# Attention with two key tiles per cycle: maxima, scores, scores, maxima on TensorE

## The chip, the core and the metric

One core of one Trainium2 chip runs the whole program. The metric is the device time of one execution in microseconds (us). The engines are TensorE (PE, with its weight loads listed as PEld), VectorE (DVE), ScalarE (ACT), GpSimd (POOL) and SyncE (SP), which here issues every DMA. Each engine runs its own queue in order and waits on semaphores for the others.

## The reference

Block-sparse attention with 4 batches of 8 heads, 768 positions and a head size of 64, followed by a feed-forward layer over the 3072 tokens:

```python
scores = scale * np.matmul(q, k.transpose(0, 1, 3, 2))      # 768 x 768 per head
scores = np.where(mask, scores, -1000000000.0)              # window, first/last and sampled blocks of 32
scores = scores - np.max(scores, axis=-1, keepdims=True)
attn = np.exp(scores)
attn = attn / (np.sum(attn, axis=-1, keepdims=True) + 1e-09)
x = np.matmul(attn, v)                                      # heads side by side: 3072 x 512
h = x @ w_in                                                # 512 -> 2048
out = (h - np.tanh(h)) @ w_out                              # 2048 -> 512
```

## The kernel before

The 32 heads are worked in 16 pairs, since two heads of 64 fill 128 partitions. A head has six tiles of 128 keys. float32 accuracy comes from high and low parts (hi and lo), and the mask is put into the products by 24 more rows of the operands: `slot` buffers, three of them, hold keys and queries with those rows, and row 88 holds the negated maximum of each query.

For a pair, `prep_qk` transposes keys and queries on PE (`ptk`, `ptq`, L205), ACT makes the hi part (`hik`, `hiq`, L207), DVE the lo part (`lok`, `loq`, L208), and `dist` sends them into the slot by DMA (L220). `prep_v` scales the values: a maximum on DVE (`am`), a product on PE (`pa`, L240), three small DVE steps (`sb`), the hi part on ACT (`vhl`, L250) and the lo part on DVE (`vhl`, L251), which reads ACT's.

For a head, six calls of `smax` compute approximate scores with queries on partitions (`sm`, L265, two matmuls) and DVE reduces each to a column of `mc` (L269). `smax_fin` transposes `mc` on PE (`pmt`, L274), DVE negates it (`nm`, L276), and a DMA puts it into the slot (L277). Then come six calls of `qk_exp`: the exact scores with keys on partitions (`st`, four matmuls, L293 and L294; L294 reads the maxima), and the exponential on ACT (`pe`, L297). `split` makes a float16 hi part (`ph`, ACT L307, at two tiles of twelve DVE L305) and a lo part (`pl`, POOL L309, at one tile of twelve DVE). `accum` multiplies with the values, 18 small matmuls per tile (`av`, L324, L332, L333), always for two tiles in a row. `norm` divides (`rs`, `xq`), `spill` writes the pair to HBM.

All of `sm`, `st`, `ptk`, `ptq` live in one PSUM pool of three wide buffers (`ps_big`, two banks each). A tile gets one that is free at its place in the schedule, and which one is fixed in the built program. `pa`, `pmt` and `av` share two small ones.

The order of the work is a table of times: `at(time, f, ...)` enters each call with a time in units of one key tile, the list is sorted, and the calls are made in that order. A scheduler then orders each engine's queue; from head 5 on (`CH0`) a chain of dependencies, `in_order`, keeps `sm`, `st` and `av` on PE in the order of the calls. For key tile i = 6h + t, `qk_exp` stands at i, `smax` at i + TSM (up to one unit later in the first heads, `ramp`), `split` at i + 2.1, and the two `accum` of an even tile and its successor at i + 5.19 and i + 5.2. `smax` therefore runs ten tiles ahead, in the next pair of heads.

After the last pair the feed-forward part (class `FFN`) runs: `first` (L548), the activation, and `second` (L580 to L582).

Of the kernel before, what the change touches and what calls it, by code (L numbers as in the profile page):

```python
# [54 lines left out]
X0, DX = 175, 2  # L55


TQK, TV, TSM, LSP, LAV = -15.1, -5.6, -9.95, 2.1, 4.2
CH0 = 5
HPH, HPL = 29, 30  # L60
RS, RQ, RV, HR = 1, 2.5, 3, 6
# [15 lines left out]
@with_exitstack  # L77
def attention_ffn(ctx, tc, q, k, v, samp, w_in, w_out, blocks, out):
    nc = tc.nc
    cst = ctx.enter_context(tc.tile_pool(name="cst", bufs=1))  # L80
    dpool = ctx.enter_context(tc.tile_pool(name="dpool", bufs=1, space=DRAM))
    xscr = [dpool.tile([P, T, DM], F32, name=f"xscr{b}") for b in range(B)]

    ident = cst.tile([P, P], F32, name="ident")
    make_identity(nc, ident)
    bias = [cst.tile([P, 1], F32, name=f"bias{i}") for i in range(2)]
    for x, val in zip(bias, (QB, THR2)):
        nc.vector.memset(x, val)

    slots = [cst.tile([P, 4, 2, S], F32R, name=f"slot{i}") for i in range(NSLOT)]  # L90
    wt = {(m, ft): dpool.tile([P, 512], F32, name=f"w{m}{ft}") for ft in range(NPRE) for m in "io"}
    part = [dpool.tile([P, DM], F32, name=f"part{j}") for j in range(CT)]
    f2 = ctx.enter_context(tc.tile_pool(name="f2", bufs=2))
    stage = [cst.tile([P, 1024], I32, name=f"stage{i}") for i in range(2)]
    ffn = FFN(tc, w_in, w_out, xscr, ident, bias, slots, wt, out, f2, part, stage)
    with ExitStack() as actx:
        big = actx.enter_context(tc.tile_pool(name="ps_big", bufs=3, space=PSUM))
        one = actx.enter_context(tc.tile_pool(name="ps_one", bufs=2, space=PSUM))
        ps = (
            lambda name: big.tile([P, 1024], F32, tag="big", name=name),  # L100
            lambda name: one.tile([P, 512], F32, tag="one", name=name),
        )
        ffn.big, ffn.one = ps
        attention(actx, tc, q, k, v, samp, w_in, w_out, blocks, xscr, ident, ps, slots, wt, f2, ffn)
    with ExitStack() as fctx:
        ffn.rest(fctx)


def attention(ctx, tc, q, k, v, samp, w_in, w_out, blocks, xscr, ident, ps, slots, wt, f2, ffn):
# [247 lines left out]
    def ramp(h, by):  # L357

        return by * max(0, 1 - (h - 1) / HR) if h else 0

    def at(time, f, *args):
        ev.append((time, len(ev), f, args))
# [36 lines left out]
    for h in range(2 * NPAIR):  # L399
        tsm = TSM + ramp(h, RS)  # L400
        for t in range(T):
            i = 6 * h + t
            at(i + tsm, smax, h, t)
            at(i, qk_exp, h, t)
            at(i + LSP, split, h, t)
            at(i + LAV + PAIR * (1 - t % 2), accum, h, t)
        at(6 * h + tsm + 5.05, smax_fin, h)
        at(6 * h + 5 + LAV + 0.05, norm, h)
# [283 lines left out]
```

## Time and profile before

| | |
|---|---|
| three runs, median (lowest to highest) | 985.94 us (982.2 to 987.58) |
| the profiled execution's time | 984.79 us |
| its span, first to last instruction | 983.0 us |
| mean granted TensorE clock | 0.979 |
| busy: PE, PEld, DVE, ACT, POOL | 922.7, 770.8, 731.5, 630.0, 458.6 us |
| chain that ended last, share by engine | PE 73%, DMA 8%, ACT 6%, DVE 5% |
| first products of the feed-forward part | 429.92 us |

A row of a timeline is: start, duration, engine, line, operation, output<-inputs, shapes, count, and in brackets the idle time of the engine before it with what ended it. A matmul's duration includes its way through the array, so the time that it keeps PE is read from start to start. A row of waits is: who waited for whom, total us, times, longest. A row of the chain of waits is: start, duration, what.

### The profile page before, as it was taken

The page shows a single profiled execution, that of the slowest core. Times are in us where ns is not written, and L with a number is a line of the kernel's source. Part 1 is how long each engine was busy: PE and PEld are TensorE (multiplying, and loading weights), DVE is VectorE, ACT ScalarE, POOL GpSimd, SP SyncE. Part 2 cuts the span into 40 slices and gives each one's busy share as a digit, 9 for nine tenths or more (in the row PEclk, how much of TensorE's full clock was granted, in tenths as well). Part 3 has the DMA queues.
Part 4 walks back from the last instruction along what each step waited for, and adds up shares of the span by engine and source line. Part 5 has one row for each costly group of instructions (what it writes and reads, how often), then busy time and mean ns, then how long its engine had stood idle before and what let it go on. Part 6 is the DMA issues. An engine that isn't in the chain of part 4 may idle for free.

```text
span 983.0 us, 18553 instructions
## 1 busy us (share of the span) xinstructions
PE 922.7 (94%) x7264; PEld 770.8 (78%) x7264; DVE 731.5 (74%) x1120; ACT 630.0 (64%) x943; POOL 458.6 (47%) x308
## 2 busy tenths in 40 slices
PE   5789899999999999878999999999999999999997
PEld 3677788888887888767788888888888888888885
DVE  5679778888887888869999876765676666566664
ACT  1566878888888888665666665555555465555553
POOL 1556767777777777854445422222222222222221
PEclk9788999999999999998999999999999999999999
DMA  9896767777776767215451220210020000001001
GB/s 234 197 288 177 191 145 173 169 165 170 166 172 157 165 156 189 72 37 168 149 169 48 65 76 11 97 33 12 1 75 1 1 33 11 1 1 44 1 1 43
DMA packets 74695, 99.78 MB, mean 102 GB/s; under 512 B 6008, under 2 KB 63544, under 8 KB 74608
## 3 DMA queue, kind: packets, MB, share of 16 engines
q1 hardware_dynamic: 74608, 98.60, 38.5%
q8 instruction: 57, 0.93, 0.4%
q14 instruction: 30, 0.25, 0.1%
HBM read 44.64 MB, written 15.20 MB: 61 GB/s over the span
## 4 chain that ended last, share of the span: by engine, by line
PE 73%; DMA 8%; ACT 6%; DVE 5%; issue 4%; SPq 2%; POOL 1%; ACTq 0%; DVEq 0%; POOLq 0%
PE pf L548 25%; PE pf L580 9%; PE pf L581 8%; PE pf L582 8%; PE st L293 5%; PE st L294 5%; PE sm L265 4%; ACT pe L297 3%; DMA slot<-lok 2%; PE av L324 2%; PE av L332 2%; PE av L333 2%; DMA slot<-nm 2%; DMA rawi<-w_in 1%; SPq L220 1%
## 5 line engine op out<-in xcount | busy, mean ns | idle before, releaser
L309 POOL TENSOR_TENSOR pl<-pe,ph 128x768 f16<-128x768 f32 x173 | 290.4, 1693 | 130.9 <-ACT ph L307 63.8
L571 POOL TENSOR_TENSOR gl<-t,gh 128x512 fp32r<-128x512 f32 x96 | 124.3, 1295 | 357.4 <-ACT gh L570 305.3
L269 DVE TENSOR_REDUCE mc<-sm 128x1 f32<-128x768 f32 x192 | 181.1, 952 | 54.3 <-PE sm L265 51.5
L297 ACT ACTIVATE pe<-st 128x768 f32<-128x768 f32 x192 | 154.4, 806 | 81.6 <-PE st L294 71.2
L293 PE MATMUL st<-slot 128*128 128x512 f32 (+1 forms) x384 | 146.9, 383 | 17.6 <-ACT pe L297 13.4
L563 DVE TENSOR_TENSOR t<-t,pf 128x512 f32<-128x512 f32 x94 | 64.6, 688 | 122.8 <-ACT t L557 122.7
L570 ACT ACTIVATE gh<-t 128x512 fp32r<-128x512 f32 x96 | 60.6, 631 | 120.7 <-DVE t L567 120.7
L307 ACT ACTIVATE ph<-pe 128x768 f16<-128x768 f32 x154 | 130.0, 844 | 4.7
L294 PE MATMUL st<-slot 89*128 89x512 f32 (+1 forms) x384 | 126.8, 350 | 1.4 <-DMA slot<-nm 1.4
L265 PE MATMUL sm<-slot 88*128 88x512 f32 (+1 forms) x384 | 111.2, 376 | 11.1 <-DMA slot<-hiq 5.4
L324 PE MATMUL av<-vhl,ph 128*128 128x65 f16 x1152 | 120.8, 195 | 0.0
L333 PE MATMUL av<-vhl,pl 128*128 128x65 f16 x1152 | 119.6, 194 | 1.0 <-POOL pl L309 1.0
L332 PE MATMUL av<-vhl,ph 128*128 128x64 f16 x1152 | 119.8, 196 | 0.0
L324 PEld LDWEIGHTS <-ph 128*128 128x128 f16 x1152 | 106.8, 97 | 13.7 <-issue 13.0
L333 PEld LDWEIGHTS <-pl 128*128 128x128 f16 x1152 | 107.9, 100 | 3.1 <-issue 1.7
L332 PEld LDWEIGHTS <-ph 128*128 128x128 f16 x1152 | 108.0, 98 | 0.6 <-issue 0.5
L555 ACT ACTIVATE u<-pf 128x512 f32<-128x512 f32 x94 | 56.2, 598 | 81.3 <-PE pf L548 81.0
L293 PEld LDWEIGHTS st<-slot 128*128 128x128 f32 x384 | 75.3, 196 | 35.9 <-ACT pe L297 18.5
L294 PEld LDWEIGHTS st<-slot 89*128 89x128 f32 x384 | 75.9, 198 | 11.9 <-DMA slot<-nm 2.8
L265 PEld LDWEIGHTS sm<-slot 88*128 88x128 f32 x384 | 62.8, 203 | 18.9 <-issue 5.8
L567 DVE COPY_PREDICATED t<-mk,pf 128x512 f32<-128x512 int32 x94 | 69.9, 744 | 6.9 <-DVE pf L566 0.5
L581 PE MATMUL pf<-wx,gh 128*128 128x512 f32 x192 | 74.7, 389 | 0.0
(123 smaller groups left out, 1962.7 us busy)
## 6 DMA issues: line engine op xcount, KB each, us to landing
slot<-hik SPq DMA_DIRECT2D x64, 192.0 KB
slot<-hiq SPq DMA_DIRECT2D x64, 192.0 KB
stage<-w_in SPq DMA_DIRECT2D x13, 512.0 KB
stage<-w_out SPq DMA_DIRECT2D x13, 512.0 KB
rawk<-k SPq DMA_DIRECT2D x16, 384.0 KB
rawq<-q SPq DMA_DIRECT2D x16, 384.0 KB
slot<-lok SPq DMA_DIRECT2D x32, 192.0 KB
slot<-loq SPq DMA_DIRECT2D x32, 192.0 KB
```

Of the source, the lines that this page charges most:

```text
L265: nc.tensor.matmul(pm[:, c], lhsT=sB[s][0:88, j, t * P : (t + 1) * P], rhs=sA[s][0:88, j, c], start=True, stop=True)
L269: maxed.append(nc.vector.tensor_reduce(out=mcs[h][:, t : t + 1], in_=pm[:, 0:S], op=ALU.max, axis=AX.X))
L293: ms.append(nc.tensor.matmul(st[:, c], lhsT=sC[s][:, j, kc], rhs=sD[s][:, j, c], start=True, stop=False))
L294: ms.append(nc.tensor.matmul(st[:, c], lhsT=sA[s][0:89, j, kc], rhs=sB[s][0:89, j, c], start=False, stop=True))
L297: nc.scalar.activation(out=pe, in_=st[:, 0:S], func=AF.Exp, scale=0.125)
L307: nc.scalar.activation(out=ph, in_=pe, func=AF.Copy)
L309: d = eng.tensor_tensor(out=pl, in0=pe, in1=ph, op=ALU.subtract)
L324: m = nc.tensor.matmul(o[:, to, :], lhsT=ph[:, c], rhs=vv[:, 0:65], start=(kt == 0 and t == 0), stop=False, skip_group_check=True)
L332: nc.tensor.matmul(o[:, to, 0:64], lhsT=ph[:, c], rhs=vv[:, 65:129], start=False, stop=False, skip_group_check=True)
L333: m = nc.tensor.matmul(o[:, to, :], lhsT=pl[:, c], rhs=vv[:, 0:65], start=False, stop=last, skip_group_check=True)
L548: nc.tensor.matmul(h, lhsT=w[:, cc], rhs=x[:, c, :], start=(k == 0), stop=(k == 3 * NCT - 1))
L581: nc.tensor.matmul(o, lhsT=gh[:, c], rhs=wo[1][ft], start=False, stop=False)
```

## The change

Two numbers: TSM, which places `smax`, goes from -9.95 to -9.0, and odd tiles get 0.05 less, even ones 0.05 more. In a stretch of two key tiles the calls were scores, maxima, scores, maxima, products; now they are maxima, scores, scores, maxima, products, and each maximum, with `smax_fin` behind it, stands 0.95 later (0.9 or 1.0 by parity).

```diff
-TQK, TV, TSM, LSP, LAV = -15.1, -5.6, -9.95, 2.1, 4.2
+TQK, TV, TSM, LSP, LAV = -15.1, -5.6, -9.0, 2.1, 4.2
...
-            at(i + tsm, smax, h, t)
+            at(i + tsm + (-0.05 if i % 2 else 0.05), smax, h, t)
```

PE in the steady part, from the transposed queries of pair 9 on (st_4 and st_5 are scores of head 15, sm_n maxima of head 17; in brackets the semaphores waited for). Before:

```order
L205 MATMUL ptq_3882<-ident,rawq_3238 128x128 [waits DMAHW4_49,DVE_49]
L205 MATMUL ptq_3882<-ident,rawq_3238 128x128 x5
L293 MATMUL st_4_3902<-slot_74 128x512 [waits Activation_49]
L294 MATMUL st_4_3902<-slot_74 128x512
L293 MATMUL st_4_3902<-slot_74 128x256
L294 MATMUL st_4_3902<-slot_74 128x256
L265 MATMUL sm_2_3909<-slot_75 128x512 [waits DVE_49]
L265 MATMUL sm_2_3909<-slot_75 128x256
L293 MATMUL st_5_3921<-slot_74 128x512 [waits Activation_49]
```

Now:

```order
L205 MATMUL ptq_3878<-ident,rawq_3238 128x128 [waits DMAHW4_49,DVE_49]
L205 MATMUL ptq_3878<-ident,rawq_3238 128x128 x5
L265 MATMUL sm_1_3894<-slot_75 128x512 [waits Activation_49]
L265 MATMUL sm_1_3894<-slot_75 128x256
L293 MATMUL st_4_3902<-slot_74 128x512 [waits DVE_49]
L294 MATMUL st_4_3902<-slot_74 128x512
L293 MATMUL st_4_3902<-slot_74 128x256
L294 MATMUL st_4_3902<-slot_74 128x256
L293 MATMUL st_5_3917<-slot_74 128x512 [waits DVE_49]
L294 MATMUL st_5_3917<-slot_74 128x512
L293 MATMUL st_5_3917<-slot_74 128x256
L294 MATMUL st_5_3917<-slot_74 128x256
```

The two score tiles now follow each other, with a maximum ahead of them, and st_5 waits for DVE where it waited for ACT. By the banks of the built program st_5 had st_4's buffer and now has that of sm_1; ptq had that of sm_1 and now has that of sm_0, which stands ahead of the products in both.

DVE at the same place, from the last maximum of head 16 to the lo part of the keys. Before:

```order
L269 TENSOR_REDUCE mc_3574<-sm_5_3746 128x1
L242 TENSOR_REDUCE sb_3733<-pa_3731 128x1
L269 TENSOR_REDUCE mc_3802<-sm_0_3803 128x1
L245 TENSOR_SCALAR sb_3733<-sb_3733 128x1
L276 TENSOR_SCALAR nm_3756<-pmt_3754 6x128
L248 TENSOR_SCALAR sb_3733<-sb_3733 128x1
L269 TENSOR_REDUCE mc_3802<-sm_1_3831 128x1
L208 TENSOR_TENSOR lok_3812<-ptk_3813,hik_3811 128x768
L251 SCALAR_TENSOR_TENSOR vhl_105<-rawv_2765,sb_3733,vhl_105 128x12x64
```

Now:

```order
L269 TENSOR_REDUCE mc_3585<-sm_5_3786 128x1
L248 TENSOR_SCALAR sb_3729<-sb_3729 128x1
L276 TENSOR_SCALAR nm_3799<-pmt_3797 6x128
L251 SCALAR_TENSOR_TENSOR vhl_105<-rawv_2765,sb_3729,vhl_105 128x12x64
L269 TENSOR_REDUCE mc_3826<-sm_0_3827 128x1
L208 TENSOR_TENSOR lok_3807<-ptk_3808,hik_3806 128x768
```

The lo part of the values, vhl, stood behind the reduces of sm_0 and sm_1 and now stands ahead of both. On ACT, where vhl's hi part is made, the order was pe_2, ph_2, hik, vhl, pe_3 and is now pe_2, vhl, hik, ph_2, pe_3; in the tile pairs without such work it was pe, ph, pe, ph and is now pe, pe, ph, ph.

DVE at the start, from the reduces of heads 0 and 1 on (nm_205 and nm_215 are head 0's). Before:

```order
L269 TENSOR_REDUCE mc_218<-sm_1_223 128x1
L276 TENSOR_SCALAR nm_205<-pmt_203 6x128
L231 TENSOR_REDUCE am_208<-rawv_172 128x1
L269 TENSOR_REDUCE mc_218<-sm_2_240 128x1
L208 TENSOR_TENSOR lok_228<-ptk_229,hik_227 128x768
L242 TENSOR_REDUCE sb_212<-pa_210 128x1
L208 TENSOR_TENSOR loq_245<-ptq_246,hiq_244 128x768
```

Now:

```order
L269 TENSOR_REDUCE mc_218<-sm_1_223 128x1
L231 TENSOR_REDUCE am_203<-rawv_172 128x1
L208 TENSOR_TENSOR lok_228<-ptk_229,hik_227 128x768
L208 TENSOR_TENSOR loq_241<-ptq_242,hiq_240 128x768
L242 TENSOR_REDUCE sb_207<-pa_205 128x1
L276 TENSOR_SCALAR nm_215<-pmt_213 6x128
L269 TENSOR_REDUCE mc_218<-sm_2_260 128x1
```

Head 0's negated maxima stand behind the work on the first values and on pair 1. Further on, the first step of converting a weight tile (cvti, L447) stood behind head 2's nm and the first two reduces of head 3 and now stands ahead of them.

## The prediction

> **What bounds the kernel now.** I read the stretches first, then what TensorE (PE) waits for, then the instructions of one cycle. The stretches (columns: stretch and length in us; busy time and count on PE, weight loads, VectorE (DVE), ScalarE (ACT), GpSimd (POOL); granted clock; DMA share; GB/s), under a row of the chain of waits with the first products of the feed-forward part:
>
> ```profile
> 429.92 2.97 PE h L548 x12
> 0.00:40.00 40.00, 22.53 (x85) 16.77 (x86) 20.96 (x36) 10.73 (x13) 9.23 (x12) 0.87 0.91 218
> 230.00:280.00 50.00, 47.55 (x628) 40.95 (x627) 40.32 (x65) 41.86 (x54) 37.95 (x24) 1.00 0.69 160
> 480.00:983.00 503.00, 495.67 (x2211) 408.35 (x2209) 349.83 (x530) 282.80 (x492) 139.42 (x108) 1.00 0.12 39
> ```
>
> Attention ends near 430 us; the rest is the feed-forward part, from 480 us on 495.67 of 503 us PE, which the change does not touch. In steady attention PE is busy 47.55 of 50 us and the other engines at most 84%. So a microsecond that PE waits longer in attention moves the end by one, and at most 5% of that stretch can be gained. What PE waited for, 80 to 400 us (total us, times, longest):
>
> ```profile
> PE st L293 <- ACT pe L297: 11.2, 13, 1.0
> PE sm L265 <- DMA slot<-lok: 3.4, 3, 1.8
> PE st L294 <- DMA slot<-nm: 0.6, 2, 0.4
> ```
>
> One wait of scores (st) on the exponential (pe) occurs 13 times: once per pair of heads, which holds 12 key tiles. The rest is small. On PE the wait stands here:
>
> ```profile
> 253.87 0.82 PE L205 MATMUL ptk<-ident,rawk 128*128 128x128 f32 x6
> 254.52 0.27 PE L274 MATMUL pmt<-ident,mc 128*6 128x128 f32 x1
> 254.55 0.48 PE L293 MATMUL st<-slot 128*128 128x512 f32 x1
> ...
> 255.34 0.51 PE L265 MATMUL sm<-slot 88*128 88x512 f32 x2
> 255.69 0.21 PE L324 MATMUL av<-vhl,ph 128*128 128x65 f16 x1
> ...
> 256.77 0.19 PE L333 MATMUL av<-vhl,pl 128*128 128x65 f16 x1
> 256.90 0.87 PE L205 MATMUL ptq<-ident,rawq 128*128 128x128 f32 x6
> 257.53 0.48 PE L293 MATMUL st<-slot 128*128 128x512 f32 x1
> ...
> 258.32 0.51 PE L265 MATMUL sm<-slot 88*128 88x512 f32 x2
> 259.78 0.50 PE L293 MATMUL st<-slot 128*128 128x512 f32 x1 [0.95 <-ACT pe L297]
> ```
>
> Starts give the time each piece keeps PE: scores of a key tile 0.79 (254.55 to 255.34), maxima 0.35, ptk 0.65, pmt 0.03, ptq 0.63, products of two tiles with the gap behind them 1.21 (255.69 to 256.90). The wait, counted from where st could have started (258.32 + 0.35), is 1.11; the 0.95 in the row counts from the modelled end of the matmul. The other engines at that place:
>
> ```profile
> 255.83 0.93 ACT L250 ACTIVATE vhl<-rawv,sb 128x768 f16<-128x768 f32 x1
> 258.93 0.80 ACT L297 ACTIVATE pe<-st 128x768 f32<-128x768 f32 x1
> 260.85 0.81 ACT L297 ACTIVATE pe<-st 128x768 f32<-128x768 f32 x1 [1.12 <-PE st L294]
> 261.69 0.84 ACT L307 ACTIVATE ph<-pe 128x768 f16<-128x768 f32 x1
> ...
> 255.88 0.96 DVE L269 TENSOR_REDUCE mc<-sm 128x1 f32<-128x768 f32 x1 [0.56 <-PE sm L265]
> 256.76 0.95 DVE L208 TENSOR_TENSOR lok<-ptk,hik 128x768 fp32r<-128x768 f32 x1
> 257.62 1.01 DVE L251 SCALAR_TENSOR_TENSOR vhl<-rawv,sb,vhl 128x768 f16<-128x768 f32 x1
> 258.55 0.16 DVE L342 SCALAR_TENSOR_TENSOR rs<-av,sb 128x6 f32<-128x6 f32 x1
> 262.64 1.52 DVE L309 TENSOR_TENSOR pl<-pe,ph 128x768 f16<-128x768 f32 x1 [0.15 <-ACT ph L307]
> ```
>
> Key tile 4's exponential ends at 259.73 and key tile 5's scores start at 259.78: they wait for that very buffer (the built program puts both into the same PSUM banks). There are three wide PSUM buffers; each st, sm, ptk, ptq takes one until ACT or DVE has read it. The transposed queries (ptq) keep theirs until DVE's lo part is made, so near them only two turn.
>
> **The change, part by part.** The counts of instructions stay; the change moves them. Handoffs that I need: st start to its exponential 1.07 (259.78 to 260.85); exponential end to PE 0.05; sm start to its reduce 0.54 (255.34 to 255.88); reduce end to PE 0.06 (256.84 to 256.90).
>
> *Removed.* Tile 5's scores no longer follow tile 4's exponential. Gain: 1.11, and about 0.07 of waiting ahead of ptq (256.84 against the products' end): 1.18 per pair.
>
> *Added, first: ptq.* By the banks of the built program ptq takes the buffer of the next pair's first maxima tile (sm tile 0), which PE issues one product pair earlier. On DVE that tile's reduce now stands behind vhl, which needs ACT's vhl, which needs ACT's exponential of tile 2 to be through. From the start of tile 2's scores: 1.07 to the exponential, 0.84 until ACT's next instruction, 0.93 for vhl on ACT, 0.11 to DVE (261.69 + 0.84 to a start on DVE at 262.64), 0.93 for vhl on DVE (257.62 to 258.55), 0.96 for the reduce, 0.06 to PE: 4.90. PE's own way to ptq is 0.79 + 0.65 + 0.03 + 0.79 + 0.35 + 1.21 = 3.82. Wait: 1.08, or 0.9 if PE's pieces run a little longer; I take 1.00. Behind ptq stand sm tile 1, scores 4 and 5 and all later PE work; ACT's hiq and its next exponential wait for them.
>
> *Added, second: tile 5 again.* It now takes the buffer of sm tile 1, which is given just ahead of tile 4's scores. Its reduce ends 0.54 + 0.96 + 0.06 = 1.56 after sm's start; PE is there after 0.35 + 0.79 = 1.14. Wait 0.42.
>
> *Added, third: scores back to back.* With tiles 0 and 1 of the odd head's successor in a row, sm tile 4 behind them takes tile 0's buffer: 1.07 + 0.81 + 0.05 = 1.93 against 2 x 0.79 = 1.58. Wait 0.35, less 0.05 where scores take longer. The other places have at least 1.7 us of PE work between (a product pair and a maximum, or a score tile more) and cost nothing.
>
> Sum: 1.00 + 0.40 + 0.30 = 1.70 added, 1.18 removed, +0.5 per pair. Low, 0.85 + 0.35 + 0.25: +0.3; high, 1.08 + 0.55 + 0.35: +0.8. There are 13 such pairs (pairs 3 to 15 are prepared inside the fixed PE order): **+6.5 us** (3.5 to 10.5).
>
> *Moved: exponentials in pairs.* ACT now runs pe, pe, ph, ph. That puts the first ph some 0.8 later for POOL, whose result the products take two pairs of tiles later: about 2 us of room remain, so nothing; without that room 0.8 per pair.
>
> *Moved: the maxima, a key tile later.* The row of negated maxima (nm) goes to SBUF by DMA and scores wait for it at L294:
>
> ```profile
> 315.82 0.27 PE L274 MATMUL pmt<-ident,mc 128*6 128x128 f32 x1
> 322.26 0.50 PE L294 MATMUL st<-slot 89*128 89x512 f32 x1 [0.18 <-DMA slot<-nm]
> 316.89 0.27 DVE L276 TENSOR_SCALAR nm<-pmt 6x128 fp32r<-6x128 f32 x1
> 317.19 5.02 DMA slot<-nm
> 207.99 2.32 DMA slot<-nm
> ```
>
> From pmt to that L294 PE had 6.26 us of work (322.26 - 0.18 - 315.82). Now it has 0.03 + 3 x 0.35 + 2 x 1.21 + 2 x 0.79 + 0.35 + 0.31 (L293 to L294) = 5.74, 0.5 less; but nm stood 1.07 behind pmt because sm tile 0's reduce was ahead of it on DVE, and now it stands ahead of that reduce, some 0.35 behind pmt. The 0.7 covers the 0.5: nothing. Without it, 0.5 at each of 13 even heads, +6.5. pmt itself waits for the last reduce, 1.56 after sm; PE has 1.79 between: nothing.
>
> *Moved: first maxima of a new pair.* They waited for key and query parts by DMA (3.4 us in three waits). From ptq to that sm PE had 0.63 + 5 x 0.79 + 4 x 0.35 + 2 x 1.21 and the wait of 1.11, 9.5 us; now 0.63 + 6 x 0.79 + 5 x 0.35 + 2 x 1.21 + 0.03 and waits of 0.7, 10.3. On SP a lo transfer moves behind the queries' first hi part. Each wait shrinks by 0.8 or goes: **-2.5 us** (0 to -3.4).
>
> *Start.* The scheduler changes the order freely until head 5. Before:
>
> ```profile
> 21.65 0.26 DVE L276 TENSOR_SCALAR nm<-pmt 6x128 fp32r<-6x128 f32 x1
> 27.40 0.95 DVE L231 TENSOR_REDUCE am<-rawv 128x1 f32<-128x768 f32 x1 [5.49 <-DMA rawv<-v]
> 23.79 7.06 DMA slot<-nm
> 30.89 0.79 PE L294 MATMUL st<-slot 89*128 89x512 f32 x1 [0.83 <-DMA slot<-nm]
> 50.22 0.27 DVE L276 TENSOR_SCALAR nm<-pmt 6x128 fp32r<-6x128 f32 x1
> 54.01 0.43 DVE L447 TENSOR_SCALAR cvti<-rawi 128x512 int32<-128x512 int32 x1 [2.09 <-DMA rawi<-w_in]
> 57.81 0.80 PE L293 MATMUL st<-slot 128*128 128x512 f32 x1 [2.37 <-DVE lok L208]
> ```
>
> Now head 0's nm stands on DVE behind am, lok, loq and sb: 27.40 + 3 x 0.87 + 0.2 = 30.2 instead of 21.65, with SP's later issues queued behind its DMA. It lands at 30.5 + 2.32 = 32.8 at best, 37.5 with the 7.06 of the crowded queue, against 30.85: 2.0 to 6.7 late. Part is repaid, since L293 of three tiles and two maxima run during the wait. And cvti, which waits for a weight load until 54.01, now stands ahead of head 2's nm and two reduces, so that nm leaves after 56 rather than 50.5. Both lie in one chain; I take **+2.5** (0 to 6).
>
> Sum: 6.5 - 2.5 + 2.5 = +6.5 on the profiled execution's 984.79, whose span is 983.0: 991.3. That execution lies 1.15 below the median of the three runs, 985.94, inside their spread (982.2 to 987.58); I leave it so.
>
> **A rule to weigh.** In the first 40 us the granted clock is 0.87 in the mean. Behind the wait that ends at 57.81 the fourth matmul of the score tile starts 1.24 later, where a whole tile took 0.79 in the steady part:
>
> ```profile
> 59.05 0.42 PE L294 MATMUL st<-slot 89*128 89x256 f32 x1
> ```
>
> The Trainium skill, "TensorE: Matmul & The Clock Gate", Part 1, The HAM clock gate, says that an idle window of about 3.4 us puts the array back to half rate and a busy one releases it. The trace agrees in direction: slow behind the long waits of the start, 1.00 in the steady part with its 1 us waits. By that rule the three short waits cost no clock, and a second long wait at the start would.
>
> **Rivals.** (1) No change: the three new waits come out at their low sums (+3.5), the DMA waits vanish (-3.4), the start repays itself: 985 to 989. For it: the steady difference is only half a microsecond per pair. Against: the ptq wait follows from fixed orders. (2) Faster: the reduce of sm tile 0 is not held, because vhl is done earlier on ACT than I read. Then 0.70 is added against 1.18 removed, 13 x -0.48 = -6, with -2.5 and a start of +1: 977. It decides where vhl ends on ACT within 3.82 - 2.06 = 1.8 us of the start of tile 2's scores; ACT's order puts it at 2.84. (3) Much slower through the start: a second stretch at the low clock, five score tiles at 0.67 more (1.24 and about 0.22 for the fourth matmul, less 0.79), 3.4, and nm 6 late: 997 to 999. For it, the 7.06 row. (4) nm late in steady state: if the reduce of sm tile 5 is held on DVE, scores of the next even head wait 0.5, 13 times: 998. Against: 0.6 us of such waiting now.
>
> **How the numbers follow.** Forecast 0.48 (989 to 995), no change 0.26, faster 0.12, start 0.09, nm 0.05. A measurement of this kernel tells about 0.5%, 4.9 us: slower means above 990.9. Of the forecast 0.36 lies above that, with (3) and (4) 0.50; faster, below 981, 0.12; the rest 0.38. Range 982 to 998: it leaves out (2) and the far ends of (3) and (4); the likeliest case alone spans 989 to 995.
>
> **What would show it.** PE: ptq waiting about 1 us for DVE's mc, 13 times; st behind mc about 0.4; sm behind pe about 0.3; the 1.0 us waits of st on pe gone; waits on slot<-lok below 1.5 in all. At the start, head 0's first L294 at 32 to 34 us. The time of a pair of heads half a microsecond longer. I am wrong if ptq does not wait, or if head 10 or so is reached no later than before.

## The result and the profile after

The changed kernel takes 997.74 us (median of four runs, 995.04 to 1001.64). The kernel before, run beside it, takes 986.29 (982.2 to 987.58). The ratio is 1.0126, with a 95% interval of 1.0092 to 1.0159: slower by 11.5 us. The forecast was 991.3, 5 us above the same kernel before (its sum was +6.5 on the profiled execution; the two profiled executions, 984.79 and 995.04, differ by 10.25). The direction was right and the value lies just inside the range, but the loss is more than double the forecast. So the question is what the sum had left out.

The stretches of the kernel after, first and last as in the prediction (columns as there; the last begins 10 us later because everything does):

```profile
0.00:40.00 40.00, 21.64 (x64) 15.06 (x65) 19.57 (x35) 9.15 (x12) 5.96 (x10) 0.69 0.92 215
230.00:280.00 50.00, 46.57 (x624) 40.22 (x621) 42.63 (x62) 39.04 (x51) 36.40 (x23) 1.00 0.70 164
490.00:993.00 503.00, 496.05 (x2214) 408.94 (x2212) 349.61 (x530) 283.16 (x492) 139.26 (x108) 1.00 0.12 39
```

The feed-forward part is what it was. In the steady part of attention PE is busy a microsecond less in 50, and VectorE, which was given no work, is busy 2.3 us more (42.63 against 40.32). Fewer pieces of work in 50 us and a busier engine: some instruction on VectorE has become longer. What PE waits for, 80 to 400 us (total us, times, longest):

```profile
PE ptq L205 <- DVE mc L269: 8.5, 11, 0.8
PE st L293 <- DVE mc L269: 7.9, 22, 0.7
PE sm L265 <- ACT pe L297: 3.4, 13, 0.4
PE st L293 <- ACT pe L297: 2.1, 2, 1.1
PE st L294 <- DMA slot<-nm: 1.1, 2, 0.8
```

The old wait of scores on pe is nearly gone (2.1 us in 2, before 11.2 in 13), and the waits on slot<-lok are gone altogether (before 3.4). In their place stand the three forecast waits, but one of them, scores on a reduce, comes 22 times, not 11. The length of a pair of heads can be read from ScalarE's key parts (hik, one per pair). First the kernel before, then the one after (least, median and longest ns, then the first and the last start):

```profile
L207 ACT ACTIVATE hik<-ptk x11: 792/792/793, 136.1 to 375.9; 128x768 fp32r<-128x768 f32 x11
```

```profile
L207 ACT ACTIVATE hik<-ptk x11: 790/794/797, 139.3 to 384.7; 128x768 fp32r<-128x768 f32 x11
```

Ten pairs take 239.8 us before and 245.4 after: 23.97 and 24.54 each. Before, six of the ten pairs were lengthened by irregular waits (the trace has 1.7 us on slot<-lok in these ten pairs, 0.2 on nm and 0.9 with no releaser); an undisturbed one took 23.53:

```profile
136.13 0.79 ACT L207 ACTIVATE hik<-ptk 128x768 fp32r<-128x768 f32 x1
159.66 0.79 ACT L207 ACTIVATE hik<-ptk 128x768 fp32r<-128x768 f32 x1
```

So the steady cost is 1.0 us per pair, twice the 0.5 that was forecast, and some 0.44 per pair of irregular waits (4.4 in the ten) went away. The span grew by 10.3 us: 3.2 up to the first of these pairs, 5.6 in the ten, and 1.5 behind them.

One pair on PE:

```profile
262.04 0.21 PE L324 MATMUL av<-vhl,ph 128*128 128x65 f16 x1
264.10 0.88 PE L205 MATMUL ptq<-ident,rawq 128*128 128x128 f32 x6 [0.79 <-DVE mc L269]
265.17 0.40 PE L293 MATMUL st<-slot 128*128 128x512 f32 x1
266.38 0.50 PE L293 MATMUL st<-slot 128*128 128x512 f32 x1 [0.35 <-DVE mc L269]
267.55 0.20 PE L324 MATMUL av<-vhl,ph 128*128 128x65 f16 x1
268.67 0.59 PE L265 MATMUL sm<-slot 88*128 88x512 f32 x2
269.10 0.40 PE L293 MATMUL st<-slot 128*128 128x512 f32 x1
269.81 0.40 PE L293 MATMUL st<-slot 128*128 128x512 f32 x1
270.93 0.62 PE L265 MATMUL sm<-slot 88*128 88x512 f32 x2 [0.25 <-ACT pe L297]
...
277.77 0.51 PE L265 MATMUL sm<-slot 88*128 88x512 f32 x2
...
279.67 0.40 PE L293 MATMUL st<-slot 128*128 128x512 f32 x1
280.89 0.50 PE L293 MATMUL st<-slot 128*128 128x512 f32 x1 [0.34 <-DVE mc L269]
```

Counted from start to start, as in the prediction: products take 1.12 where nothing waits (267.55 to 268.67), ahead of ptq 2.06, so ptq waits 0.94. A score tile takes 0.71 where another piece follows at once (269.10 to 269.81); the second of two follows 1.21 behind the first at 265.17 and 1.22 at 279.67, a wait of 0.50 each; and sm follows 1.12 behind 269.81, a wait of 0.41. Together 2.35 per pair, where 1.70 was forecast. Less the 1.18 removed, that is 1.17; 0.16 of it comes back in PE's own pieces: a score tile with another right behind it takes 0.71 where one took 0.79 before, which is more than the maxima behind products lose (0.43 at 268.67, before 0.35). The wait at 280.89 is the one that the prediction does not have. VectorE and GpSimd (POOL) there:

```profile
262.14 1.04 DVE L251 SCALAR_TENSOR_TENSOR vhl<-rawv,sb,vhl 128x768 f16<-128x768 f32 x1 [0.69 <-ACT vhl L250]
263.10 0.94 DVE L269 TENSOR_REDUCE mc<-sm 128x1 f32<-128x768 f32 x1
...
267.57 0.55 DVE L305 CAST ph<-pe 128x768 f16<-128x768 f32 x1
...
276.56 0.96 DVE L269 TENSOR_REDUCE mc<-sm 128x1 f32<-128x768 f32 x1
...
278.17 1.80 DVE L305 CAST ph<-pe 128x768 f16<-128x768 f32 x1 [0.19 <-ACT pe L297]
279.88 1.81 DVE L269 TENSOR_REDUCE mc<-sm 128x1 f32<-128x768 f32 x2
```

```profile
268.20 1.64 POOL L309 TENSOR_TENSOR pl<-pe,ph 128x768 f16<-128x768 f32 x1 [1.27 <-DVE ph L305]
...
276.28 3.26 POOL L309 TENSOR_TENSOR pl<-pe,ph 128x768 f16<-128x768 f32 x2 [0.57 <-POOL pl L309]
```

VectorE makes ph by a CAST for two of the 12 key tiles of a pair. The one of the odd head, at 267.57, takes 0.55 with GpSimd idle. The one of the even head's tile 4, at 278.17, takes 1.80, and it ends at 279.97, 0.43 behind the end of GpSimd's two pl (276.28 + 3.26 = 279.54). The reduces behind it are late, and the scores with them. Of the kernel before, the same CAST and GpSimd's row ahead of it:

```profile
271.88 0.55 DVE L305 CAST ph<-pe 128x768 f16<-128x768 f32 x1
```

```profile
268.42 3.46 POOL L309 TENSOR_TENSOR pl<-pe,ph 128x768 f16<-128x768 f32 x2 [0.23 <-POOL pl L309]
```

There the two pl end at 271.88, where the CAST starts. It was not always so: of the ten even heads' CASTs in that part of the kernel before, five took 0.86 and one 0.59, each begun before GpSimd's two pl had ended. One of them, with its row on GpSimd (end 152.70; the CAST ends at 153.12):

```profile
152.26 0.86 DVE L305 CAST ph<-pe 128x768 f16<-128x768 f32 x1
```

```profile
149.43 3.27 POOL L309 TENSOR_TENSOR pl<-pe,ph 128x768 f16<-128x768 f32 x2 [0.23 <-ACT ph L307]
```

So the old trace held the sign of it. The new order makes the exponentials in pairs, so that GpSimd's pl come in pairs behind them, and the CAST falls into the second of two. That GpSimd is the cause is, so far, only read from two ends that lie near each other; the first two experiments test it.

### The profile page after: what moved, and what is told of

Read it like the earlier page. It is cut to its first block, busy times and chain, and to the rows that moved or that the text cites. A ratio compares the mean times of both kernels' runs of the same rounds, so it can differ in the third digit from the quotient of the medians.

```text
span 993.3 us, 18569 instructions
## 1 busy us (share of the span) xinstructions
PE 923.3 (93%) x7264; PEld 768.5 (77%) x7264; DVE 749.3 (75%) x1120; ACT 620.9 (63%) x943; POOL 454.7 (46%) x308
## 4 chain that ended last, share of the span: by engine, by line
PE 73%; DVE 13%; DMA 5%; ACT 4%; issue 3%; SPq 1%; ACTq 0%; DVEq 0%
PE pf L548 25%; PE pf L580 8%; PE pf L581 8%; PE pf L582 8%; PE sm L265 5%; DVE mc L269 5%; PE st L293 5%; PE st L294 4%; ACT pe L297 3%; DVE ph L305 2%; PE av L324 2%; PE av L332 2%; PE av L333 2%; DMA rawi<-w_in 1%; DMA slot<-nm 1%
## 5 line engine op out<-in xcount | busy, mean ns | idle before, releaser
L309 POOL TENSOR_TENSOR pl<-pe,ph 128x768 f16<-128x768 f32 x173 | 286.6, 1673 | 144.6 <-ACT ph L307 92.9
L297 ACT ACTIVATE pe<-st 128x768 f32<-128x768 f32 x192 | 151.0, 809 | 88.9 <-PE st L294 88.0
L293 PE MATMUL st<-slot 128*128 128x512 f32 (+1 forms) x384 | 138.3, 365 | 20.7 <-DVE mc L269 13.4
L307 ACT ACTIVATE ph<-pe 128x768 f16<-128x768 f32 x154 | 125.3, 840 | 1.9
L265 PE MATMUL sm<-slot 88*128 88x512 f32 (+1 forms) x384 | 114.7, 385 | 10.9 <-DMA slot<-hiq 5.5
```

The costliest lines, as they stand in the source:

```text
L265: nc.tensor.matmul(pm[:, c], lhsT=sB[s][0:88, j, t * P : (t + 1) * P], rhs=sA[s][0:88, j, c], start=True, stop=True)
L293: ms.append(nc.tensor.matmul(st[:, c], lhsT=sC[s][:, j, kc], rhs=sD[s][:, j, c], start=True, stop=False))
L297: nc.scalar.activation(out=pe, in_=st[:, 0:S], func=AF.Exp, scale=0.125)
L307: nc.scalar.activation(out=ph, in_=pe, func=AF.Copy)
L309: d = eng.tensor_tensor(out=pl, in0=pe, in1=ph, op=ALU.subtract)
```

## The experiments

All ran in five rounds beside the kernel before, whose median on that chip was 984.88 to 986.13 us. Steady pair and place are worked out from the hik rows as above (mean of ten pairs, and the start of the first of them, which tells how much everything ahead of it took). The intervals of e1 and e3 touch that of the change; there the pair and the place carry the reading:

| kernel | us | ratio to before [95%] | pair | place |
|---|---|---|---|---|
| before | 986.29 | 1 | 23.97 | 136.1 |
| the change | 997.74 | 1.0126 [1.0092, 1.0159] | 24.54 | 139.3 |
| e1: CAST on ScalarE | 993.19 | 1.0090 [1.0058, 1.0122] | 24.10 | 138.3 |
| e11: GpSimd idle at the CAST | 991.09 | 1.0057 [1.0038, 1.0077] | 23.95 | 142.7 |
| e7: V projection earlier | 990.42 | 1.0048 [1.0025, 1.0070] | 24.08 | 136.9 |
| e3: old start | 992.47 | 1.0080 [1.0048, 1.0112] | 24.53 | 134.5 |
| e6: new order alone | 998.88 | 1.0132 [1.0107, 1.0157] | 24.64 | 139.6 |
| e5: delay alone | 999.14 | 1.0142 [1.0097, 1.0186] | 24.53 | 144.1 |
| e12: change + e1 + e7 | 979.10 | 0.9928 [0.9902, 0.9954] | 23.10 | 136.2 |
| e14: e12 + old start of heads 0, 1 | 976.04 | 0.9889 [0.9858, 0.9919] | 23.10 | 134.2 |
| e8: e12 + old start of heads 0 to 5 | 973.67 | 0.9878 [0.9850, 0.9907] | 23.10 | 132.4 |
| e9: before + e1's edit | 992.86 | 1.0074 [1.0046, 1.0103] | 24.03 | 139.9 |
| e10: before + e7's edit | 989.42 | 1.0034 [1.0011, 1.0057] | 23.93 | 139.9 |
| e13: before + both | 981.97 | 0.9957 [0.9936, 0.9977] | 23.55 | 132.1 |

**e1: the CAST taken off VectorE.** On the changed kernel:

```
-PH_DVE = (4, 10)
+PH_DVE = (10,)
```

> The changed kernel with one edit: the float16 hi part of key tile 4 of even heads is made by ACT and no longer by a CAST on DVE (that of odd heads stays on DVE). Theory of the CAST: in the changed kernel this CAST takes 1.80 us instead of 0.55 at 12 places, because it falls into POOL's work on pl; the reduce behind it (mc) is late and scores of tile 1 of the next odd head wait. Without it a pair of heads falls from 24.5 us to about 24.0, there is one wait of st on mc per pair instead of two, and the time goes from 997.7 to about 992. Rival: that wait comes from DVE's load or the order of the maxima; then the pair stays at 24.5, and 0.84 us more on ACT per pair bring nothing or a little loss, 997 to 999.

993.19 us, 4.5 less than the change; the usual pair is 23.93 (one of the ten is 25.46, with a wait for nm). PE's waits, 80 to 400 us:

```profile
PE ptq L205 <- DVE mc L269: 10.6, 11, 1.1
PE st L293 <- DVE mc L269: 8.7, 13, 4.2
```

The second wait of scores on a reduce is gone (13 times in place of 22, one of them the 4.2 of the start, which the change has too, at 79.0, just outside the window). So the unforecast 0.50 came from this CAST. Start to start, the tile that waited then took 0.86 and the maxima behind it 0.45 in the change; here they take 0.71 and 0.35, so the CAST cost 0.75 per pair in all. Part of the gain went back: ptq waits 10.6 in place of 8.5, 0.18 per pair start to start.

**e11: GpSimd idle while the CAST runs.** This run keeps the CAST where it is and takes GpSimd's work away from it: pl of tile 3 of even heads is not made. Its products with V read ph a second time, so the numbers that come out are others, while PE does the same number of products.

```
...
+        if h % 2 == 0 and h < HPH and kt == 3:
+            plin[h, kt] = d
+            phs[h, kt] = ph, ph
+            return
         eng = nc.vector if (h * T + kt) % 12 in (PL_DVE if h < HPL else PL_DVE_END) else nc.gpsimd
         d = eng.tensor_tensor(out=pl, in0=pe, in1=ph, op=ALU.subtract)
```

> The changed kernel without GpSimd's pl of key tile 3 in even heads (the products with V take ph in its place, so the low part of that tile is not computed: this run leaves out work). The CAST of key tile 4 stays on VectorE and starts at the same place, only GpSimd is idle there for the last 1.65 us. Theory (the CAST is held until the second of two pl that stand back to back on GpSimd has ended): the CAST ends 0.4 us behind the end of the first one instead and takes 0.55 to 0.7 us; the second wait of the scores for the reduce of the maxima goes from 0.50 to under 0.1 us, the pair of heads from 24.53 to 23.9 to 24.1 us, the time to 991 to 994 us. Rival (the CAST is long by what it reads, or by its place behind the maxima, and GpSimd only ends near it by chance): it stays at 1.8 us, pair 24.5, 996 to 999 us.

991.09 us, pair 23.95. The CAST, and GpSimd ahead of it (line numbers are a little higher in this kernel):

```profile
278.83 0.56 DVE L306 CAST ph<-pe 128x768 f16<-128x768 f32 x1 [0.19 <-ACT pe L297]
```

```profile
276.95 1.66 POOL L314 TENSOR_TENSOR pl<-pe,ph 128x768 f16<-128x768 f32 x1 [0.56 <-POOL pl L314]
279.47 3.26 POOL L314 TENSOR_TENSOR pl<-pe,ph 128x768 f16<-128x768 f32 x2 [0.87 <-DVE ph L306]
```

GpSimd is free from 278.61, and the CAST at 278.83 takes 0.56 with the same operands, the same neighbours on VectorE and the same releaser. The rival falls: what makes the CAST long is GpSimd's work beside it. The steady pair (23.95) is the mean of e1 without its one long pair (23.95), as it should be if both take away the same wait.

**e7: the wait of ptq.** The V projection, whose VectorE part (vhl) stands ahead of the reduce that ptq waits for, is given three key tiles earlier:

```
-TQK, TV, TSM, LSP, LAV = -15.1, -5.6, -9.0, 2.1, 4.2
+TQK, TV, TSM, LSP, LAV = -15.1, -8.6, -9.0, 2.1, 4.2
```

> The changed kernel with the preparation of the values three key tiles earlier (TV -8.6 instead of -5.6). In the built order vhl on ACT and DVE then lies ahead of the tiles that prepare keys and queries. Theory of the ptq wait: ptq waited 0.8 to 0.9 us per pair for the reduce that vhl held up; it waits under 0.3 now, a pair takes about 23.5 us, and the time is 985 to 988. Rival: the wait moves, since lok now stands ahead of that reduce on DVE and hik still waits on ACT: pairs of 24.2 to 24.5, 994 to 998.

990.42 us, 7.3 less than the change, pair 24.08, both between what the theory and the rival had. The waits, 80 to 400 us:

```profile
PE st L293 <- DVE mc L269: 3.8, 11, 0.4
...
PE ptk L205 <- DVE mc L269: 1.8, 11, 0.2
```

The wait of ptq, the largest forecast term, is gone, and so it did come from vhl. The pair falls by 0.46 only, half of that wait: ptk now waits for a reduce (start to start the score tile ahead of it takes 1.04 in place of 0.71, and ptk 0.86 in place of 0.66), and the CAST is still held by GpSimd:

```profile
249.83 1.40 DVE L305 CAST ph<-pe 128x768 f16<-128x768 f32 x1
```

**e3: the start.** Maxima of heads 0 to 5, and the loads tied to them, at the times of the kernel before, on the changed kernel:

```
-        tl = TSM + ramp(NMH - 1, RS) + 6 * NMH + 0.1 * pr
+        tl = -9.95 + ramp(NMH - 1, RS) + 6 * NMH + 0.1 * pr
...
-        tsm = TSM + ramp(h, RS)
+        tsm = (TSM if h >= 6 else -9.95) + ramp(h, RS)
...
-            at(i + tsm + (-0.05 if i % 2 else 0.05), smax, h, t)
+            at(i + tsm + ((-0.05 if i % 2 else 0.05) if h >= 6 else 0), smax, h, t)
```

> The changed kernel, with the maxima of heads 0 to 5 at the times that they had before (TSM -9.95, no parity), and the new times from head 6 on; the loads keep their old times. Theory that the start costs some 3 us (late maxima of head 0, the weight conversion ahead of them on DVE): 994 to 995, pairs of the steady part unchanged at 24.5 us, hik of pair 5 near 136 us instead of 139. Rival that the start repays itself and all of the loss is in the steady part: 997 to 998.

992.47 us, 5.3 less than the change; the pair is the same (24.53) and its place 4.8 earlier, more than the 3 us that I expected. But this place, 134.5, is also 1.6 earlier than that of the kernel before (136.1). So 4.8 is what the old times are worth in the new kernel; against the kernel before, which is what the prediction spoke of, the change's place is 3.2 later.

**e6 and e5: order and delay apart.** e6 has the new order at the old times (TSM -10.0 with the shifts of 0.05 exchanged). e5 has the old order, maxima a key tile later (TSM -8.95, no shifts).

> The kernel of the change with its new order (maxima, scores, scores, maxima, then the products with V) but without the delay: every key tile's maxima are given at the old time, not one key tile later. Theory (the loss is made by the order: the evictions of the V projection stand ahead of a reduce, and the CAST of even heads' key tile 4 runs into GpSimd): what counts is which instructions are neighbours on VectorE, so a shift of one key tile puts the maxima's pair beside other work; the loss should then be of another size, I estimate 985 to 992 us, with the projection of pe's partner work no longer waiting for the reduce next to the V evictions (under 0.3 us of waiting per pair there instead of 0.92). Rival (the delay is harmless and the order alone costs all of it): 996 to 999 us, pair of heads 24.5 us. Second rival (the delay alone costs, at the start and through nm): 983 to 987 us, with the waits of the first maxima for the DMA of lok back at about 3 us.

> The kernel before with one number: TSM -8.95, so the order scores, maxima, scores, maxima, products stays and the maxima are one key tile later. Theory that the lateness itself costs nothing in the steady part: pairs of 23.5 us with the 1 us wait of st on pe still there, waits on DMAs smaller, and only a late start: 986 to 990. Rival that the lateness is the cost (maxima row late for the scores, conversions ahead of the maxima): pairs of 24 us and more with waits at L294, 994 to 998.

Neither is cheap: 998.88 and 999.14, each as much as both together, and both outside what I had as theory. In the steady part e6 shows what the change shows, without any delay, as its first rival had it. Its waits, 80 to 400 us:

```profile
PE st L293 <- DVE mc L269: 10.5, 21, 3.3
PE ptq L205 <- DVE mc L269: 8.5, 11, 0.8
```

e5 shows another kernel: the old wait is still there, and rows of maxima (nm) are late.

```profile
PE st L293 <- ACT pe L297: 11.4, 13, 0.9
PE st L294 <- DMA slot<-nm: 5.9, 8, 1.6
```

So the steady loss of the change belongs to its order. The delay by itself costs in another way, ahead of the first place (144.1) and through nm; the mean pair is 24.53 here too, but the single pairs vary from 23.69 to 26.71. That the new order makes room for nm is only read from its 1.1 us of such waits.

e6 also parts the start. Its nm of heads 0 and 2 leave at 21.99 and 50.43, as before, and the key part of pair 2 starts at 53.2 (before 52.5, the change 56.0). So most of the lateness at that point belongs to the delay. Its late place, 139.6, is lost further on, between pairs 3 and 4, with a wait of 3.3 us of scores on a reduce at 106 us.

**e8: the three repairs together.** e3, e1 and e7 in one kernel, with the new order.

> The three edits that each took back a part, together, on the changed kernel: maxima of heads 0 to 5 as before the change, the CAST of even heads' key tile 4 on ScalarE, and the V projection three key tiles earlier. Theory (the loss is three separate terms: a start of about 5 us, a CAST behind GpSimd, a wait of the projection for a reduce): the pair of heads falls from 24.53 to 23.4 to 23.6 us, which is that of the kernel before without its DMA waits, and the time is 979 to 984 us, level with the kernel before or up to 0.6% faster. Rival (the terms are one and the same slack: what one edit frees, the next wait takes): pair 23.9 to 24.1 us, 985 to 989 us.

973.67 us, below all that was expected, and 1.2% faster than the kernel before. The pair is 23.10, 1.44 below that of the change, while e1 alone saved 0.61 (its usual pair) and e7 0.46: each alone had moved a part of its wait to another place. The largest wait that is left, 80 to 400 us:

```profile
PE st L293 <- DVE mc L269: 8.7, 14, 0.9
```

**e12 and e14: what of it is the start.** e12 is e8 without the edit of the start; in e14 only heads 0 and 1 have the old one (`h >= 2` for `h >= 6`).

> The kernel of 973.67 us without its edit of the start: the changed kernel with the CAST of even heads' key tile 4 on ScalarE and the V projection three key tiles earlier, maxima one key tile later from head 0 on. Theory (the late maxima cost about 5 us at the start, apart from the other two terms): 978 to 981 us, pair of heads 23.1 us. Rival (the start's loss comes from those same two waits in its first heads and is gone with them): 973 to 975 us. Second rival (the early maxima are what made the pair shorter than the sum of the single edits): pair 23.4 to 23.6 us, 982 to 986 us.

> The kernel of 973.67 us, with the old times of the maxima only for heads 0 and 1 (there: heads 0 to 5); heads 2 to 5 get theirs a key tile later and in the new order. Of the 5.4 us that the start costs (979.10 against 973.67) this tells which part is head 0's row of maxima standing behind the maximum of V, and which is what follows, the row of head 2 behind the conversion of a weight that waits for its load. Theory (head 0 is most of it, its first scores with the row come at 34.0 instead of 29.8 us): 973.5 to 976 us. Rival (the later heads are most of it): 977 to 980 us.

979.10 and 976.04. The pair is 23.10 in all three, so the edit of the start is worth 5.4 us in the medians here too (3.8 in the place), apart from the other terms. Of these, 3.1 seem to go to heads 0 and 1 and 2.4 to heads 2 to 5, but the interval of e14 overlaps both others; that split is not settled. The first scores that need head 0's nm, in e8 and in the change (forecast for 32 to 34 us):

```profile
29.83 0.79 PE L294 MATMUL st<-slot 89*128 89x512 f32 x1 [0.55 <-DMA slot<-nm]
```

```profile
35.02 0.79 PE L294 MATMUL st<-slot 89*128 89x512 f32 x1 [0.20 <-DMA slot<-nm]
```

**e9, e10 and e13: the same edits in the old order.** On the kernel before: e9 has e1's edit, e10 has e7's, e13 both.

> Control on the kernel before: the CAST of even heads' key tile 4 on ScalarE, nothing else changed. Theory (in the kernel before this CAST takes 0.55 to 0.86 us and no maxima wait behind it): within 0.3% of the kernel before, 982 to 988 us. Rival (VectorE is simply too full in both kernels, and taking 0.55 us of it helps either alike): about as much faster as the same edit made the changed kernel, 4.5 us, so 979 to 982 us.

> Control on the kernel before: the V projection three key tiles earlier, nothing else changed. Theory (the projection waits for a reduce only in the changed kernel, 0.92 us per pair against 0.09): no gain, 983 to 989 us. Rival (the earlier V projection is good by itself, whatever the order of the maxima): as much faster as in the changed kernel, 7 us, so 976 to 980 us.

> The kernel before, in its old order, with the two steady edits of the kernel of 973.67 us: the CAST of even heads' key tile 4 on ScalarE, and the V projection three key tiles earlier. Theory (in the old order the scores wait about 1 us per pair for the exponential ahead of them, and neither edit takes that away; each alone cost 3 to 7 us): 988 to 996 us, so the new order is needed for the gain. Rival (the two edits together free the engines whatever the order): 972 to 978 us, and the new order is worth nothing.

Alone each makes the old kernel slower (992.86 and 989.42); the first I had not expected, the second is just above my 983 to 989. Together they make it faster by 0.4%, which neither theory had (I expected 988 to 996). In e9 and e10 the mean pair is 24.03 and 23.93, as before, though in e10 every pair takes it: the irregular waits are gone and small steady ones came (maxima on a reduce, 4.0 us in 12 between 80 and 400 us, and products on xq, 2.5 in 11). What they lose lies outside: the place is 3.8 later, with one wait of this kind near 87 us, here in e9 (and the stretch behind the ten pairs is 3.1 us longer in e9 and 2.2 in e10, which nothing here explains):

```profile
86.83 0.38 PE L274 MATMUL pmt<-ident,mc 128*6 128x128 f32 x1 [2.97 <-DVE mc L269]
```

With both edits the pair is 23.55 in the old order and 23.10 in the new one: the old order keeps its wait on pe.

```profile
PE st L293 <- ACT pe L297: 8.7, 13, 1.3
```

So the new order does gain 0.45 us per pair once these two collisions are taken out. The intervals of e13 (0.9936 to 0.9977) and e8 (0.9850 to 0.9907) do not meet; that of e12, which has the new order from head 0 on (0.9902 to 0.9954), overlaps e13's.

## Why the prediction was right in sign and wrong in size

By the steps of its sum, per pair of heads where nothing else is said:

| step | forecast | measured |
|---|---|---|
| removed: tile 5 behind tile 4's exponential | 1.18 less | gone |
| ptq behind the reduce that vhl holds | 1.00 | 0.94 |
| tile 5 behind a reduce | 0.40 | 0.50 |
| sm tile 4 behind tile 0's exponential | 0.30 | 0.41 |
| "The other places ... cost nothing" | 0 | 0.50 (0.75 with the longer pieces behind it) |
| undisturbed pair | +0.5 | +1.0 |
| DMA waits of the first maxima, in all | -2.5 | irregular waits, about -4.4 in ten pairs |
| start, in all | +2.5 | +3.2 (place, against the kernel before) |

- **The step that failed** is "The other places have at least 1.7 us of PE work between ... and cost nothing". At the place that failed PE has even 2.61 between (277.77 to 279.67 + 0.71). The way from sm's start to PE over the reduce is 1.56, so either would have covered it had VectorE been free. I gave each VectorE instruction the duration of its row before the change and did not ask what would run on GpSimd beside it. The CAST of the even head grew from 0.55 to 1.80, and the reduces behind it were late. e1 and e11 each take this away by another road and arrive at the same pair. In eleven pairs (22 waits of both kinds) 0.50 is 5.5 us; the forecast of 991.3 was 6.4 us below the median and 3.7 below the profiled execution.
- **The three forecast waits** came at the places named and within 0.11 us of their size. That ptq's comes from vhl is shown by e7; for the other two there is only the trace.
- **The start** came out near its forecast of +2.5: against the kernel before, the change is 3.5 us late at pair 2 (its hik at 55.98, before at 52.49) and 3.2 at the first of the ten pairs, which has some steady loss in it. Both mechanisms named are in the trace: head 0's nm leaves VectorE late, and head 2's stands behind cvti.

```profile
31.91 0.27 DVE L276 TENSOR_SCALAR nm<-pmt 6x128 fp32r<-6x128 f32 x1
54.35 1.08 DVE L447 TENSOR_SCALAR cvti<-rawi 128x512 int32<-128x512 int32 x1 [0.81 <-DMA rawi<-w_in]
57.62 0.27 DVE L276 TENSOR_SCALAR nm<-pmt 6x128 fp32r<-6x128 f32 x1
```

  The prediction had 30.2 and "after 56". The 5.3 of e3 and 5.4 of e12 and e8 are larger in part because they are counted from e3 and e8, which reach that place 1.6 and 3.7 us earlier than the kernel before. How much of the start is the named rows and how much the scheduler's other choices there stays open: e9 and e10, which leave the maxima's times alone, also moved the place by 3.8 us, and e11, which differs from the change by one subtraction per pair, by 3.4.
- **Steady nm: nothing**, as forecast (1.1 us in 2). e5 shows that this holds for the new order only; in the old one the same delay costs 5.9 us of waiting for nm. Waits of the kind that rival 4 names are real, in another kernel than this one.
- **Rival 1** (no change) needed the small sums and a start that repays itself; neither came. **Rival 2** (vhl early on ScalarE) falls by the row at 262.14: VectorE waited 0.69 for ScalarE's half. **Rival 3** (997 to 999) has the measured time inside it, but not by what it named: the start lost 3.2, and between 40 and 90 us the granted clock was 0.90 in the change and 0.86 before, so there was no second stretch at a low clock.

  In the first 40 us the change's clock was low (0.69). Yet e7, which has the same first maxima, ran there at 1.00 and reached pair 2 no earlier, at 57.12 us against 55.98:

```profile
0.00:40.00 40.00, 21.38 (x64) 14.73 (x64) 19.07 (x35) 8.66 (x11) 5.47 (x10) 1.00 0.93 217
```

- **The tail** behind the last of these pairs is 1.5 us longer in the profiled run of the change. Among the kernels of the table that stretch varies between 607 and 611 us. I take it as spread.

The forecast itself held as to why the change does not pay: it trades a wait on ScalarE's exponential for waits that are mostly on VectorE. What it missed is that VectorE's own durations move with the order. That the time still lies inside the range is in part luck: the irregular waits gave back 1.9 us more than the sum had. The runs also correct the verdict on the order: with these two collisions taken out it is the better one.

## What to carry to other kernels

When an edit changes what runs side by side, do not carry over durations from the old trace without looking at who stands beside them: here one 0.55 us instruction became 1.80, and everything queued behind it was late. The longest of its group in the old trace, 0.86, was a sign of it. When a reordering loses, look for the one or two instructions that it collides with before giving it up; taking out one alone may only move the wait to the other (0.61 and 0.46 us per pair saved apart, 1.44 together). And test repairs against the old order too, with the steady cycle read apart from the start: in e9 and e10 the mean cycle was as before and the loss lay ahead of it and behind it.

## What the runs showed of the hardware

An f32-to-f16 CAST from SBUF to SBUF on VectorE (128x768) took 0.55 us with GpSimd idle, and 1.80 when it came 1.4 us ahead of the end of two back-to-back GpSimd subtractions. In the steady part of the change it lasted until 0.42 us behind that end (0.43 by the rounded rows above), which is less than a free CAST takes as a whole. The same 0.41 to 0.42 stands behind every CAST of this tile that overlapped a pl in the steady parts of the kernel before, e3, e5, e6 and e7, whether it had begun 0.20 or 1.48 behind the start of that pl (1.87 and 0.59 long). The group over the steady part, before and after the change (least, median, longest ns):

```profile
L305 DVE CAST ph<-pe x20: 549/551/862, 142.1 to 368.5; 128x768 f16<-128x768 f32 x20
```

```profile
L305 DVE CAST ph<-pe x20: 547/1168/1798, 144.9 to 376.3; 128x768 f16<-128x768 f32 x20
```

The reduces from PSUM beside the same GpSimd work kept their 0.94 to 0.96 (276.56 in the change). The Trainium skill, "SBUF — State Buffer", Who interferes with whom, says that VectorE's copies and casts can run in a mode that needs the port pair it shares with GpSimd, that whichever issues first keeps it for its whole instruction while the other is blocked, and that reduces do not contend. The trace agrees: 1.80 against 0.55 for the CAST, and no change for the reduces. In which mode the CAST ran, no run here shows. By the mean of the row, the second of the two pl had started at 277.91 (276.28 + 3.26 / 2), 0.26 ahead of the CAST, and it alone held it. Had I weighed this rule against the order of the CAST and the pl before predicting, it would have spoken against the step that failed.

The granted clock of the first 40 us was 0.69 in the change and 1.00 in e7 with the same first maxima, and the start was no shorter for it.
